# Where transposes stand beside PV, when loads are issued, and how background matmuls run at the end of an attention

## The chip, the cores and the metric

The kernel runs on one core of a Trainium2 chip. The metric is the device time of one execution in microseconds (us); the median of the runs counts. The engines named here are TensorE (PE; its weight loads are PEld), VectorE (DVE), ScalarE (ACT), GpSimd (POOL) and SyncE (SP), which issues nearly all DMAs.

## What is computed

One transformer block with adaptive layer norm, all in float32, over 2048 rows of 512, with 32 heads of 16 and a hidden layer of 1792:

```python
mod = (_silu(c) @ w_mod).reshape(c.shape[0], 6, 1, -1)
sa, ca, ga, sb, cb, gb = (mod[:, 0], mod[:, 1], mod[:, 2], mod[:, 3], mod[:, 4], mod[:, 5])
h = _layernorm(x, axis=-1) * (1 + ca) + sa
x = x + ga * _A_ref(h, A_wqkv, A_wo)          # softmax attention, 32 heads, scale 1/4
h = _layernorm(x, axis=-1) * (1 + cb) + sb
x = x + gb * _B_ref(h, B_w1, B_b1, B_w2, B_b2)  # gelu between two dense layers
```

## The kernel before

**Precision and pieces.** A float32 product is made of three: each operand is split into a high and a low part, and high x high, low x high and high x low are added in PSUM. For scores the parts are stacked along the contraction, 48 rows for a head of 16 (50 for the exponent's scores, which also subtract the row maximum). So a score matmul needs only half of the array's 128 rows, and the kernel keeps two row halves of 64 busy at once: matmuls that follow each other on different halves run beside each other. In the code a half is the index `a` or `h`, 0 or 1, and rows start at `a * 64`.

**Units and half-steps.** The attention is cut into 32 units, one for 4 heads and 512 query rows; unit u covers query block u // 8 and head group u % 8. A unit has 16 chunks of 128 keys, so there are 512 half-steps, `half_step(hs)`, and half-step 16u begins unit u. In each, TensorE gets, written out by hand in program order:

- four max scores, `mx_mm` (L390), which VectorE reduces to row maxima (L395). They run 88 ahead of the rest (`LEAD`), so that a unit's maxima are known before its exponentials; `max_rows` sends them through DRAM (`m<-m` L416, then `qst<-m` L422, six ticks later) into the two extra rows of the query tile. A tick of `clock` is one exponential.
- four scores for the exponential, `exp_mm` (L642), which ScalarE evaluates (L649).
- the four PV matmuls of the step before, `pv_step` (L676), each 128 rows by 32 columns.
- background work, six half matmuls (`RUN`): a job is a group of terms that add up in one bank. `bg_mm(h)` issues one term on row half h alone (L276, called from `mm`); the other half of the same rows follows in the next half-step, on the other half of the array. A group has 24 or 36 halves. Two halves may not add to one bank at the same time, so the first of the next half-step waits for an instruction that was `saw`n after the last one: an exponential, or a read of one column of the newest score bank by VectorE (`tick`, L1115).

An ordinary half-step is thus e, mx, then six times a background half and a score of the other half, then PV. Background half h runs beside scores of half 1 - h.

**Background.** `work` yields the jobs: the rest of the QKV projections (`block0`), and for query blocks 0 to 2, as their attention comes done, the output projection, residual and second layer norm (`front`) and the MLP (`feed`, whose gelu is worked out on GpSimd with a tanh on ScalarE, L910 to L921). Block 3 can only follow the attention, in the part after the loop, which also takes what is left of block 2; there gelu is ScalarE's own function (L903). `held` keeps a job for the next half-step.

**Transposes.** V is transposed on TensorE after its projection (`turn_v`, L335, 12 times within the attention), and so are the normed rows of the second layer norm (`trans`, L874; four each for blocks 0, 1 and 2). Each is four 128 x 128 transposes into one bank, evacuated by ScalarE (L340, L876). V's and those of blocks 1 and 2 are queued in `sides`, and a half-step takes one at its start, that is right behind the PV of the half-step before. They take a bank of the ring `mx`, which has three.

**Loads.** `step_start(s)` runs once a step and issues what is due: for unit u + 2 the query tile at step 16u + 6 and four quarters of K at 16u + 6, 8, 12 and 13, for unit u + 1 two halves of V at 16u + 11 and 12.

**The attention's end.** When the 2048 max scores are out, the last 22 half-steps set `ending`: the ring of e gets five banks, and groups that begin now are run by `bg_whole`, all 128 rows in one matmul, two or three in a half-step, behind the four e, which come in pairs of both halves. What is left when the loop ends is finished behind the last PV.

Of the kernel before, what the change touches and what calls it, by code (L numbers as in the profile page):

```python
# [28 lines left out]
NKC = S // P  # L29
NG = H // 4  # L30
NU = NB * NG
# [29 lines left out]
RUN = 6  # L61
# [9 lines left out]
def block_kernel(ctx: ExitStack, tc: tile.TileContext, x, wqkv, wo, w1, b1, w2, b2, c, w_mod, out):  # L71
# [56 lines left out]
    tick = const.tile([P, 1], F32, name="tick")  # L128
# [146 lines left out]
    def mm(ps, term, i, n, r=slice(None)):  # L275
        return te.matmul(ps, term[0][r], term[1][r], start=i == 0, stop=i == n - 1)  # L276
# [354 lines left out]
    def exp_mm(a, bk="e", behind=False):  # L631

        s, p = divmod(ec[a], 2)
        while begun[0] < min(ec) // 2 + 1:
            begun[0] += 1
            step_start(begun[0] - 1)
        ec[a] += 1
        u, kc = divmod(s, NKC)
        assert u in mrows, (u, ec, xc, red, clock["t"])
        r0 = a * 64  # L640
        ps = take(bk)
        ins = te.matmul(ps, kh(u, kc // 8)[r0 : r0 + KX, p, (kc % 8) * P : (kc % 8 + 1) * P], qst[u][r0 : r0 + KX, p],  # L642
                        start=True, stop=True)
        if behind:
            tc.add_manual_dep(ins.ins, exps[-2].name, AFTER, reason="orders the slots of the exponentials")

        def act():
            t = ppool.tile([P, TB], F32, tag="p", name="p")
            op = ac.activation(t, ps, AF.Exp, scale=SCALE)  # L649
# [162 lines left out]
    def front(b, x2):  # L812
# [9 lines left out]

        def norm(t):
            xn[t] = tmp("xn")
            (gp if t < 3 else ve).tensor_scalar(
                xn[t], x2[t], mv[:, t, 0:1], rs[t], op0=ALU.subtract, op1=ALU.mult)
            later(40, lambda: gp.tensor_tensor(x2[t], x2[t], b2_b, op=ALU.add))
            if b and len(xn) == 4:
                later(9, lambda: sides.extend([lambda fc=fc: trans(fc, "mx") for fc in range(KC)]))
# [25 lines left out]
        for t in range(4):  # L855

            def evac(ps, t=t):
                y = tmp("y")
                ac.activation(y, ps, AF.Copy)

                def add():
                    gp.tensor_tensor(x2[t], y, x2[t], op=ALU.add)
                    later(4 if t < 3 else 3, lambda: stat(t))

                later(2, add)

            yield o_terms(b, t, range(KC)), "bg", evac
# [146 lines left out]
    def saw(ins):  # L1014

        if act["g"] and not act["g"]["seen"]:
            act["g"]["seen"] = ins.ins
# [18 lines left out]
            act["g"] = None  # L1036
        return act["g"] is not None

    def bg_whole():

        g = act["g"]
        terms, bk, evac = g["group"]
        if g["n"] == 0:
            g["ps"] = take(bk)
        mm(g["ps"], terms[g["n"]], g["n"], len(terms))
        g["n"] += 1
        if g["n"] == len(terms):
            evac(g["ps"])
            act["g"] = None
        return act["g"] is not None  # L1050

    held, ending = [], []

    def half_step(hs):
# [4 lines left out]
        h = hs % 2  # L1059
        if h or len(wt) < len(used) + KC:  # L1060
            wload()
        if sides:
            sides.pop(0)()
        full, turn = False, None
        if act["g"] is None:
            j = held.pop() if held else next(jobs, None)
            if callable(j):
                turn = j
                full = True
                j = next(jobs, None)  # L1070
            if callable(j):
                held.append(j)
            elif j is not None:
                act["g"] = {"group": j, "at": [0, 0], "n": 0, "seen": None, "whole": bool(ending)}
        nx = min(64 * NU, LEAD + 4 * (hs + 1))
        ne = 4 * (hs + 1)

        def x_ok(a):
            return sum(xc) < nx and xc[a] < 32 * NU
# [1 line left out]
        def e_ok(a):  # L1081
            return sum(ec) < ne and ec[a] < 2 * NU * NKC

        more = act["g"] is not None
        if more and turn:
            turn()
            turn = None
        free = not more and not full and not ending
        if more and act["g"]["whole"]:
            while sum(ec) < ne:  # L1090
                for f in [exp_mm(a) for a in range(2) if e_ok(a)]:
                    f()
            for _ in range(2 if hs % 3 else 3):
                if act["g"]:
                    bg_whole()
            more = False
        k = 0
        first = more and x_ok(1 - h) and e_ok(h)
# [25 lines left out]
        while sum(ec) < ne or sum(xc) < nx:  # L1124
            a = 0 if ec[0] <= ec[1] else 1
            fs = []
            if sum(ec) < ne:
                fs.append(exp_mm(a))
                if x_ok(1 - a):
                    fs.append(mx_mm(1 - a, "bg" if free and sum(xc) == nx - 1 else "mx"))  # L1130
                elif e_ok(1 - a):
                    fs.append(exp_mm(1 - a))
            else:
                fs += [mx_mm(i) for i in range(2) if x_ok(i)]
            for f in fs:
                f()
            if turn and sum(ec) == ne - 1:
                turn()
                turn = None
        if hs:  # L1140
            assert not turn
            assert min(ec) >= 2 * cur["pv"] + 2
            pv_step()
# [5 lines left out]
    def step_start(s):  # L1149
        u, kc = divmod(s, NKC)  # L1150
        for d in [d for d in due if d[0] <= s and all(k in stored for k in d[1])]:
            due.remove(d)
            d[2]()
        if kc == 0 and u + 2 < NU:
            g = (u + 2) % NG // 2
            due.append((16 * u + 6, [(0, g, (u + 2) // NG)], lambda: load_q(u + 2)))
            for b, n in enumerate((6, 8, 12, 13)):
                t0 = b % 2 * TB
                due.append((16 * u + n, [(1, g, b)], lambda b=b, t0=t0: load_k(u + 2, b // 2, t0, t0 + TB)))
        if kc == 0 and u + 1 < NU:  # L1160
# [9 lines left out]
    if act["g"] and not act["g"]["whole"]:  # L1170
        while bg_mm(1 - hs % 2):
            pass
    pv_step()
    while act["g"]:
        bg_whole() if act["g"]["whole"] else bg_mm(hs % 2)
    close(ppcm, vgcm)


# [128 lines left out]
```

## Time and profile before

| what | value |
|---|---|
| median of 3 runs | 1701.78 us (1700.27 to 1702.31) |
| the profiled execution's own time | 1702.86 us |
| its span, first to last instruction | 1701.1 us |
| mean granted TensorE clock | 0.996 |
| stretch ahead of the attention, 0 to 113 us: PE, DVE, ACT busy | 102.0, 100.6, 39.1 us |
| attention, 113 to 1524 us: PE, DVE, ACT, POOL busy | 1405.2, 1260.5, 1121.3, 589.5 us |
| its end without max scores, 1524 to 1579 us | 54.9, 2.1, 50.1, 34.1 us |
| behind the attention, 1579 to 1701 us | 117.0, 41.2, 26.1, 23.3 us |

In the rows of a timeline stand the start, the time from start to end, the engine, the line, the operation, out<-in, the shape (rows*columns of the array, then partitions x elements) and how many were merged; a bracket holds the idle time ahead and what ended it. A group's row has the busy time, the mean of one in ns, and the idle time ahead with what ended it. A row of the waits view has the total, the count and the longest. Matmuls overlap, so what a matmul costs is read from the distance of starts, not from its own length.

### The profile page before, as it was taken

Reading aid. Unit: us, or ns where it says so; the run is one execution under the profiler, and the core shown is the slowest. Engines: PE = TensorE matmul, PEld = TensorE weight load, DVE = VectorE, ACT = ScalarE, POOL = GpSimd, SP = SyncE. Lnnn points to the kernel's source line nnn. Section 1 sums busy time; section 2 is a strip of 40 time slices with the busy share of each in tenths; the row PEclk is TensorE's granted clock in tenths of the full one; section 3 lists DMA queues with packets and bytes.
Section 4 is the critical chain, followed back from the end, with each engine's and each line's share of the span. In section 5 each row is a group of like instructions: output and inputs, shape, how many; then the busy total and the mean of one; then the engine's idle time right before and its main releaser. Section 6 shows DMA issues by size and latency. Waiting matters only on the chain.

```text
span 1701.1 us, 32616 instructions
## 1 busy us (share of the span) xinstructions
PE 1679.1 (99%) x12097; PEld 919.4 (54%) x12097; DVE 1404.4 (83%) x2677; ACT 1236.7 (73%) x2379; POOL 701.7 (41%) x710
## 2 busy tenths in 40 slices
PE   7999999999999999999999999999999999999999
PEld 6655555555554455555545555555555555553777
DVE  7998888889889988988989888888899888870432
ACT  3358788778777788778777788778777788779131
POOL 7424443435211466316633356316523367136410
PEclk8999999999999999999999999999999999999999
DMA  8746776766457533425463354354363454332554
GB/s 289 200 141 219 228 209 205 222 191 215 129 157 213 128 99 101 107 65 158 133 166 95 94 157 120 83 132 125 107 184 84 124 145 121 68 104 94 189 168 158
DMA packets 137131, 251.91 MB, mean 148 GB/s; under 512 B 25854, under 2 KB 45324, under 8 KB 136972
## 3 DMA queue, kind: packets, MB, share of 16 engines
q1 hardware_dynamic: 135712, 248.19, 51.1%
q8 instruction: 96, 1.57, 0.4%
q10 hardware_dynamic: 1260, 1.63, 0.3%
q14 instruction: 63, 0.52, 0.1%
HBM read 188.49 MB, written 61.28 MB: 147 GB/s over the span
## 4 chain that ended last, share of the span: by engine, by line
PE 92%; DVE 4%; DMA 2%; POOL 1%; ACT 1%; issue 0%; SPq 0%; DVEq 0%; POOLq 0%; ACTq 0%
PE bg L276 38%; PE pv L676 29%; PE e L642 16%; PE mx L390 4%; DVE mxp L395 3%; PE pr L276 2%; DMA wraw<-in_A_wqkv_dram 1%; PE o L276 1%; DMA qst<-m 0%; DMA wt<-wos 0%; ACT p L649 0%; PE mx L335 0%; PE mx L874 0%; DVE hTlo L484 0%; DMA xin<-in_A_x_dram 0%
## 5 line engine op out<-in xcount | busy, mean ns | idle before, releaser
L395 DVE TENSOR_REDUCE mxp<-mx 128x1 f32<-128x512 f32 x2035 | 1285.9, 683 | 146.3 <-PE mx L390 130.2
L649 ACT ACTIVATE p<-e 128x512 f32<-128x512 f32 x2048 | 1074.2, 605 | 274.8 <-PE mx L390 234.2
L390 PE MATMUL mx<-kh,qst 48*128 48x512 f32 x2035 | 833.2, 422 | 1.8 <-DVE mxp L395 1.5
L642 PE MATMUL e<-qst,kh 50*128 50x512 f32 x2048 | 772.4, 425 | 3.9 <-ACT p L649 2.8
L642 PEld LDWEIGHTS e<-qst,kh 50*128 50x128 f32 x2048 | 336.6, 185 | 430.2 <-ACT p L649 308.1
L676 PE MATMUL pv<-p,vg 128*32 128x512 f32 x4096 | 546.8, 605 | 0.0
L390 PEld LDWEIGHTS mx<-kh,qst 48*128 48x128 f32 x2035 | 367.4, 185 | 15.9 <-DVE mxp L395 10.4
L276 PE MATMUL bg<-w,g 64*128 64x512 f32 (+1 forms) x1056 | 265.3, 390 | 0.0
L276 PEld LDWEIGHTS bg<-w,g 64*128 64x128 f32 (+1 forms) x1056 | 195.7, 186 | 28.9 <-POOL m L412 0.2
L676 PEld LDWEIGHTS pv<-p,vg 128*32 128x32 f32 x4096 | 81.4, 108 | 176.5 <-issue 165.5
L276 PE MATMUL bg<-pchi,w 64*128 64x512 f32 (+1 forms) x640 | 175.2, 392 | 0.1
L276 PE MATMUL bg<-hThi,wqkv 64*128 64x512 f32 x560 | 153.0, 392 | 0.1
L276 PEld LDWEIGHTS bg<-pchi,w 64*128 64x128 f32 (+1 forms) x640 | 117.3, 186 | 22.6 <-issue 5.4
L276 PEld LDWEIGHTS bg<-hThi,wqkv 64*128 64x128 f32 x560 | 103.8, 185 | 14.0 <-DVE tick L1115 0.4
L937 POOL TENSOR_TENSOR x<-y,x 128x512 f32<-128x512 f32 x28 | 36.0, 1285 | 166.9 <-ACT y L936 162.5
L918 POOL TENSOR_SCALAR s<-s 128x512 f32<-128x512 f32 x42 | 62.8, 1495 | 99.4 <-ACT s L916 99.3
L276 PE MATMUL bg<-pclo,w 64*128 64x512 f32 (+1 forms) x320 | 87.3, 389 | 0.0
L276 PE MATMUL bg<-hTlo,wqkv 64*128 64x512 f32 x280 | 76.5, 392 | 0.0
L911 POOL TENSOR_TENSOR s<-h 128x512 f32<-128x512 f32 x42 | 43.7, 1040 | 67.3 <-ACT h L910 67.2
L276 PEld LDWEIGHTS bg<-pclo,w 64*128 64x128 f32 (+1 forms) x320 | 58.7, 184 | 9.7 <-issue 2.2
L276 PE MATMUL bg<-wo,pchi 64*128 64x512 f32 x192 | 59.6, 390 | 0.5 <-DVE mxp L395 0.4
L276 PEld LDWEIGHTS bg<-hTlo,wqkv 64*128 64x128 f32 x280 | 51.6, 184 | 7.4
(164 smaller groups left out, 1335.5 us busy)
## 6 DMA issues: line engine op xcount, KB each, us to landing
kh<-qk SPq DMA_DIRECT2D x256, 192.0 KB
w<-w1s SPq DMA_DIRECT2D x56, 512.0 KB
w<-w2s SPq DMA_DIRECT2D x54, 512.0 KB
vg<-v SPq DMA_DIRECT2D x64, 332.0 KB
qk<-parts SPq DMA_DIRECT2D x32, 512.0 KB
qst<-qk SPq DMA_DIRECT2D x64, 192.0 KB
qk<-parts SPq DMA_DIRECT2D x32, 256.0 KB
ou<-osb SPq DMA_DIRECT2D x32, 256.0 KB
```

The costliest lines, as they stand in the source:

```text
L276: return te.matmul(ps, term[0][r], term[1][r], start=i == 0, stop=i == n - 1)
L390: te.matmul(ps, qst[u][r0 : r0 + KR, p, qc * P : (qc + 1) * P], kh(u, kr // 2)[r0 : r0 + KR, p, (kr % 2) * TB : (kr % 2 + 1) * TB], start= ...
L395: ins = ve.tensor_reduce(mxp[u][:, hc, kr : kr + 1], ps, axis=AX.X, op=ALU.max, negate=True)
L642: ins = te.matmul(ps, kh(u, kc // 8)[r0 : r0 + KX, p, (kc % 8) * P : (kc % 8 + 1) * P], qst[u][r0 : r0 + KX, p], start=True, stop=True)
L649: op = ac.activation(t, ps, AF.Exp, scale=SCALE)
L676: te.matmul(cur["ps"][32 * j : 32 * (j + 1)], vg[u][:, kc, j * VW : j * VW + 32], pt.pop(4 * s + j), start=kc == 0, stop=kc == NKC - 1)
L911: gp.tensor_tensor(s, h, h, op=ALU.mult)
L918: gp.tensor_scalar(s, s, 1.0, None, op0=ALU.add)
L937: later(4, lambda: gp.tensor_tensor(x2[t], y, x2[t], op=ALU.add))
```

## The change

**Transposes.** A half-step takes its entry of `sides` at its end, ahead of PV, and not in a half-step in which a group ended. TensorE's order in the eighth half-step, where a transpose of V (L335, four) stands beside PV (L676, four); `-` is before, `+` now:

```order
 L276 MATMUL bg<-hThi_216,wqkv_222 128x512
 L390 MATMUL mx<-kh_193,qst 128x512
-L676 MATMUL pv<-p,vg 32x512 x4
 L335 MATMUL mx<-ident,vr 128x128 x4
+L676 MATMUL pv<-p,vg 32x512 x4
 L642 MATMUL e<-qst,kh_191 128x512
 L390 MATMUL mx<-kh_193,qst 128x512
```

The four transposes moved from behind PV to ahead of it. All 12 of V and the 8 of blocks 1 and 2 move so; the four of block 0 were jobs of their own and stay.

**Halves in balance.** A group no longer starts in a half-step of h = 1 while both halves have issued equally many e; it is held for the next one. Without that rule, in such a half-step three e go to one half, and one of them is of the step after. In half-steps without background the bank `bg` is now lent to the third max score rather than the fourth.

**The attention's end.** `bg_whole` is gone. The first half-step of the end issues six e, the later ones four, so that e run two further ahead; each half-step has four background halves of half h, with an e of the other half behind each. In the last five half-steps no group begins; a fetched one is held until after the loop. VectorE reads a column of the last e's bank (`tick`) for the order of the two halves. TensorE's order in two half-steps of the end before, PV (L676), e (L642) and background (L276):

```order
L676 MATMUL pv<-p,vg 32x512 x4
L642 MATMUL e<-qst,kh_192 128x512 x4
L276 MATMUL bg<-pchi_5392,w_22651 128x512 x2
L676 MATMUL pv<-p,vg 32x512 x4
L642 MATMUL e<-qst,kh_192 128x512 x4
L276 MATMUL bg<-pchi_5392,w_22651 128x512 x3
```

And one now, with each e by its own bank's number, from the last PV matmul to the next first:

```order
L676 MATMUL pv_22433<-p_22799,vg_21764 32x512
L276 MATMUL bg_22803<-pchi0_5392,w1_21633 128x512
L642 MATMUL e_22857<-qst_21150,kh1_191 128x512
L276 MATMUL bg_22803<-pchi0_5392,w1_21633 128x512
L642 MATMUL e_22862<-qst_21150,kh1_191 128x512
L276 MATMUL bg_22803<-pchi0_5392,w1_21633 128x512
L642 MATMUL e_22867<-qst_21150,kh1_191 128x512
L276 MATMUL bg_22803<-pchi0_5392,w1_21633 128x512
L642 MATMUL e_22872<-qst_21150,kh1_191 128x512
L676 MATMUL pv_22433<-p_22826,vg_21764 32x512
```

Whole background matmuls behind the e became halves between them. There are 17 half-steps like this, then three of four e, one of two and one of none, all without background, and 24 whole matmuls (two groups) behind the last PV, where there were 10.

**Loads.** Query tile at 16u + 4, K at 16u + 5, 8, 14 and 16, V at 16u + 2 and 3. SP's order from the store of unit 24's maxima (L416) to their load (L422), before; L362 is K, L595 V, L715 and L718 the attention's sums and output, L791 weights:

```order
L416 DMA m_116<-m_17887 4x32x32 x2
L362 DMA kh_191<-qk_87 48x2x512 x2
L595 DMA vg<-v 128x664
L715 DMA dn<-ou_126 128x1x32
L718 DMA ob<-ou_126 64x1x512 x2
L791 DMA wo<-wos_135 128x1024
L362 DMA kh_191<-qk_87 48x2x512 x2
L422 DMA qst<-m_116 2x1024 x2
```

And now:

```order
L416 DMA m_116<-m_17854 4x32x32 x2
L715 DMA dn<-ou_126 128x1x32
L718 DMA ob<-ou_126 64x1x512 x2
L422 DMA qst<-m_116 2x1024 x2
L791 DMA wo<-wos_135 128x1024
L715 DMA dn<-ou_126 128x1x32
L718 DMA ob<-ou_126 64x1x512 x2
L362 DMA kh_191<-qk_87 48x2x512 x2
```

K and V moved out from between the store and the load.

**Statistics.** In blocks 1 and 2 of `front` the statistics start eight ticks behind the residual addition rather than four or three, and the fourth normalization is GpSimd's like the other three, not VectorE's.

The core of the diff:

```diff
-        ps = take(bk)
+        cur["e"] = ps = take(bk)
...
-            (gp if t < 3 else ve).tensor_scalar(
+            (gp if b or t < 3 else ve).tensor_scalar(
...
-                    later(4 if t < 3 else 3, lambda: stat(t))
+                    later(8 if b else 4 if t < 3 else 3, lambda: stat(t))
...
-        if sides:
-            sides.pop(0)()
...
-            if callable(j):
+            if callable(j) or j is not None and (hs > NU * NKC - RUN if ending else h and ec[0] == ec[1]):
                 held.append(j)
             elif j is not None:
-                act["g"] = {"group": j, "at": [0, 0], "n": 0, "seen": None, "whole": bool(ending)}
+                act["g"] = {"group": j, "at": [0, 0], "n": 0, "seen": None}
...
-        ne = 4 * (hs + 1)
+        ne = min(4 * NU * NKC, 4 * (hs + 1) + 2 * len(ending))
...
-        if more and act["g"]["whole"]:
-            while sum(ec) < ne:
-                for f in [exp_mm(a) for a in range(2) if e_ok(a)]:
+        if more and ending:
+            a = 1 - h
+            if ne - sum(ec) > 4:
+                for f in [exp_mm(i) for i in (h, a) * 2]:
                     f()
-            for _ in range(2 if hs % 3 else 3):
+            k = RUN - 2
+            while k > 0 or sum(ec) < ne:
                 if act["g"]:
-                    bg_whole()
+                    bg_mm(h)
+                if k <= ne - sum(ec):
+                    f = exp_mm(a if e_ok(a) else h)
+                    if act["g"] and sum(ec) == ne:
+                        saw(ve.tensor_copy(tick, cur["e"][:, :1]))
+                    f()
+                k -= 1
             more = False
...
-                    fs.append(mx_mm(1 - a, "bg" if free and sum(xc) == nx - 1 else "mx"))
+                    fs.append(mx_mm(1 - a, "bg" if free and sum(xc) == nx - 2 else "mx"))
...
+        if sides and not (had and act["g"] is None):
+            sides.pop(0)()
         if hs:
...
-            due.append((16 * u + 6, [(0, g, (u + 2) // NG)], lambda: load_q(u + 2)))
-            for b, n in enumerate((6, 8, 12, 13)):
+            due.append((16 * u + 4, [(0, g, (u + 2) // NG)], lambda: load_q(u + 2)))
+            for b, n in enumerate((5, 8, 14, 16)):
...
-                due.append((16 * u + 11 + h, need, lambda h=h: load_v(u + 1, h)))
+                due.append((16 * u + 2 + h, need, lambda h=h: load_v(u + 1, h)))
...
-    while act["g"]:
-        bg_whole() if act["g"]["whole"] else bg_mm(hs % 2)
...
+    for j in held:
+        do(j)
```

More of the change, by code (lines that the diff above doesn't have):

```diff
@@ L1037, in bg_mm @@
         return act["g"] is not None
[L1039 to L1050, printed above, removed]
     held, ending = [], []
@@ L1082, in e_ok @@
             return sum(ec) < ne and ec[a] < 2 * NU * NKC
-        more = act["g"] is not None
+        more = had = act["g"] is not None
         if more and turn:
@@ L1169, in block_kernel @@
         half_step(hs)
-    if act["g"] and not act["g"]["whole"]:
-        while bg_mm(1 - hs % 2):
-            pass
+    assert not act["g"]
     pv_step()
-    while act["g"]:
-        bg_whole() if act["g"]["whole"] else bg_mm(hs % 2)
     close(ppcm, vgcm)
```

## Prediction

> **What bounds the kernel now.** I read the page first.
>
> ```profile
> PE 1679.1 (99%) x12097; PEld 919.4 (54%) x12097; DVE 1404.4 (83%) x2677; ACT 1236.7 (73%) x2379; POOL 701.7 (41%) x710
> ...
> L395 DVE TENSOR_REDUCE mxp<-mx 128x1 f32<-128x512 f32 x2035 | 1285.9, 683 | 146.3 <-PE mx L390 130.2
> L649 ACT ACTIVATE p<-e 128x512 f32<-128x512 f32 x2048 | 1074.2, 605 | 274.8 <-PE mx L390 234.2
> ...
> L276 PEld LDWEIGHTS bg<-w,g 64*128 64x128 f32 (+1 forms) x1056 | 195.7, 186 | 28.9 <-POOL m L412 0.2
> ```
>
> TensorE is busy 99% of the span, so a gain must come from better packed matmuls or from its few waits. The group rows give the mean of one reduction (683 ns), one exponential (605) and one weight load of the background (186). Half-steps are the unit to count in. The timeline of TensorE shows one with four transposes of background b = 1 in it, and then an ordinary one; each ends where the next PV starts.
>
> ```profile
> 953.08 1.07 PE L676 MATMUL pv<-p,vg 128*32 128x512 f32 x8
> 954.08 0.66 PE L874 MATMUL mx<-ident,xn 128*128 128x128 f32 x4
> ...
> 956.82 1.06 PE L676 MATMUL pv<-p,vg 128*32 128x512 f32 x8
> 957.81 0.49 PE L642 MATMUL e<-qst,kh 50*128 50x512 f32 x1
> ...
> 959.34 0.40 PE L390 MATMUL mx<-kh,qst 48*128 48x512 f32 x1
> 959.66 0.64 PE L676 MATMUL pv<-p,vg 128*32 128x512 f32 x4
> ```
>
> The ordinary half-step takes 959.66 - 956.82 = 2.84 us: 0.99 from PV to the first pair of score matmuls, then pairs, then 0.32 from the last max score to PV. The one with transposes takes 3.74, so 0.90 more. TensorE's order holds 450 ordinary ones, 8 such, and 12 with V's transposes, which take 3.55:
>
> ```profile
> 133.02 1.07 PE L676 MATMUL pv<-p,vg 128*32 128x512 f32 x8
> ...
> 136.57 1.07 PE L676 MATMUL pv<-p,vg 128*32 128x512 f32 x8
> ```
>
> ScalarE's timeline in the same two half-steps says why 0.90 and not less. After PV it idles 0.78 us; with transposes there, their evacuation (0.78) stands ahead of the exponentials, the score banks come free later, and pairs fall apart.
>
> ```profile
> 954.83 0.78 ACT L876 ACTIVATE h<-mx,modc 128x512 f32<-128x512 f32 x1 [1.01 <-PE mx L874]
> 955.51 2.05 ACT L649 ACTIVATE p<-e 128x512 f32<-128x512 f32 x4
> 958.34 2.07 ACT L649 ACTIVATE p<-e 128x512 f32<-128x512 f32 x4 [0.78 <-PE mx L390]
> ```
>
> **Transposes ahead of PV.** The number of switches between row shapes stays: scores, transposes, PV, scores instead of scores, PV, transposes, scores. The price at the new place is in a stretch before the attention, where transposes follow a score and precede a matmul of PV's shape.
>
> ```profile
> 79.27 0.41 PE L390 MATMUL mx<-kh,qst 48*128 48x512 f32 x2
> 79.61 0.66 PE L335 MATMUL pr<-ident,vr 128*128 128x128 f32 x4
> 80.20 1.50 PE L232 MATMUL pr<-wm,s_m 128*32 128x512 f32 x12
> ```
>
> A score to a transpose is about 0.33, as a score to PV; the four and the switch behind them are 80.20 - 79.61 = 0.59. So the half-step becomes 2.84 + 0.59 = 3.43. The evacuation now runs while PV does, in the 0.78 us that ScalarE has. What is late next is the bank: the transposes take the score bank of three max scores ago, that is of the second max score of this half-step, and VectorE must have reduced it.
>
> ```profile
> 958.38 1.89 DVE L395 TENSOR_REDUCE mxp<-mx 128x1 f32<-128x512 f32 x3 [0.59 <-PE mx L390]
> ```
>
> Three reductions of 0.68 in 1.89 us start 0.60 apart, so the second ends at 958.38 + 0.60 + 0.68 = 959.66, and the transposes could start at 959.34 + 0.33 = 959.67. That is a tie; I put 0.03 us on it. The bounds are no wait (3.43) and the third reduction's end, 0.60 more (4.03, slower than now); I take 3.46, since the order names the second bank. V: 12 x (3.55 - 3.46) = 1.1 us. Background: 8 x (3.74 - 3.46) = 2.2 us.
>
> **Attention's end.** Here the max scores are used up. Before, e come in pairs, and then two or three background matmuls of all 128 rows:
>
> ```profile
> 1533.16 0.73 PE L642 MATMUL e<-qst,kh 50*128 50x512 f32 x4
> 1533.82 0.73 PE L276 MATMUL bg<-pchi,w 128*128 128x512 f32 x2
> 1534.48 1.06 PE L676 MATMUL pv<-p,vg 128*32 128x512 f32 x8
> ```
>
> From e to PV are 1.32 us, and with the 0.99 from PV to the next e the half-step takes 2.31, for two background matmuls. After, four half matmuls run beside four e. The first half-steps of this stretch show that pairing already:
>
> ```profile
> 1525.18 0.50 PE L276 MATMUL bg<-pchi,w 64*128 64x512 f32 x1
> 1525.18 0.49 PE L642 MATMUL e<-qst,kh 50*128 50x512 f32 x1
> 1525.52 0.39 PE L276 MATMUL bg<-pchi,w 64*128 64x512 f32 x1
> 1525.52 0.62 PE L642 MATMUL e<-qst,kh 50*128 50x512 f32 x2
> 1525.75 0.39 PE L276 MATMUL bg<-pchi,w 64*128 64x512 f32 x1
> ```
>
> First to second pair 0.34, then 0.23. So a half-step is 0.34 + 2 x 0.23 + 0.33 + 0.99 = 2.12 us. The Trainium skill ("TensorE: Matmul & The Clock Gate", Part 3, What overlaps and what doesn't) says that a weight load overlaps a running matmul only when the row group differs; four half matmuls on one half would then each show their load. These rows deny it: 1525.52 and 1525.75 lie on one half, 0.23 apart. It is a rival below.
>
> Now the sum from the first matmul behind the first PV to the first behind the last. Before it is 1579.75 - 1525.18 = 54.6 us.
>
> ```profile
> 1579.75 1.65 PE L276 MATMUL bg<-pchi,w 128*128 128x512 f32 x6
> ```
>
> After, TensorE's order has one half-step of six e (8 slots less two shared, about 2.6), 17 of 2.12 (36.0), three of four e without background (0.34 + 0.33 + 0.99 = 1.66 each, 5.0), one of two e (1.3), and PV alone twice (1.0 + 1.0): 46.9. ScalarE bounds it too, in these rows:
>
> ```profile
> 1532.63 0.70 ACT L910 ACTIVATE h<-bg,b_h 128x512 f32<-128x512 f32 x1
> 1533.20 2.62 ACT L649 ACTIVATE p<-e 128x512 f32<-128x512 f32 x5
> ```
>
> Exponentials start (2.62 - 0.60) / 4 = 0.50 apart here, (2.07 - 0.60) / 3 = 0.49 above, and an evacuation takes 0.57 of its time. 88 e x 0.49 = 43.1, eight other activations x 0.57 = 4.6, the first 0.6 late and the last PV about 1.1: 49.4 if it never idles and all of this must be done by then. Running two e ahead lets it idle little; five banks keep its backlog off TensorE. The two sums give 46.9 to 49.4, and a little above if both wait in turn; I take 48.8, gain 5.8, with 4 to 7 for the range. The added reads of a score bank (L1086 of the new kernel) are on VectorE, whose only other work here is a reciprocal; the background of the next half-step and the last exponential wait for them, but PV's 0.99 lies between. If that cover were gone, each of the 15 would cost a reduction's time at most (683 ns), 10 us in all; a copy of one column is far shorter, and I take nothing.
>
> What is not done here is done later: the order has 24 whole matmuls of two groups behind the last PV, where 10 stood, so 14 more. The chain has their price, and TensorE's timeline where the waiting part begins:
>
> ```profile
> 1619.27 78.23 PE bg L276 x336
> ```
>
> ```profile
> 1597.16 3.07 PE L276 MATMUL o<-wt,kh 128*128 128x512 f32 x11
> ```
>
> 78.23 / 336 = 0.233. From 1579.75 to the output projection at 1597.16 are 17.4 us with 70 matmuls; with 84 it is 19.6. So 2.2 are given back; 0.83 of waits in the 17.4 go, because the last groups' gelu comes from ScalarE rather than GpSimd. Net gain of the end: 5.8 - 2.2 = 3.6.
>
> **Balance, loads, statistics.** The half-step ahead of the attention's end is broken today:
>
> ```profile
> 1520.92 1.07 PE L676 MATMUL pv<-p,vg 128*32 128x512 f32 x8
> 1524.18 1.07 PE L676 MATMUL pv<-p,vg 128*32 128x512 f32 x8
> ```
>
> It takes 3.26; the new order has an ordinary one there (2.84): 0.4 saved. Two kinds of wait follow, in TensorE's timeline:
>
> ```profile
> 880.18 0.47 PE L276 MATMUL bg<-wo,pchi 64*128 64x512 f32 x1 [0.41 <-DVE mxp L395]
> ...
> 1217.05 0.47 PE L642 MATMUL e<-qst,kh 50*128 50x512 f32 x1 [1.07 <-DMA qst<-m]
> ```
>
> At 1217.05 an e of unit 24 waits for its row maxima, because groups had started on the odd half and one e came half a step early; with the pairing that is lost I count 1.5 us, and 1.07 is the lower bound. In balance that e comes later, and K, V and `wo` no longer stand between the store and this load on SP: 1.5 saved. At 880.18 a group waits 0.41 for its bank, which held the last max score; now the one before. This happens twice, and the lost pair goes with it: 0.8. VectorE waits for a GpSimd addition, twice, 0.33 each:
>
> ```profile
> 928.99 0.43 DVE L839 BATCH_NORM_STATS2 bsh<-x 128x6 f32<-128x256 f32 x1 [0.33 <-POOL x L862]
> ```
>
> Eight ticks of delay instead of four cover that: 0.5. The norm moved to GpSimd (two of 2 us, GpSimd 41% busy) costs nothing, nor do V and q loaded earlier.
>
> Sum: 1.1 + 2.2 + 3.6 + 0.4 + 1.5 + 0.8 + 0.5 = 10.1 us. The profiled execution took 1702.86 (span 1701.1), 1.1 above the median; the same off both gives 1692.8 there, and a predicted median of 1701.78 - 10.1 = 1691.7.
>
> **Rivals.** (a) Transposes bound: the 0.90 and 0.71 are the matmuls' own, or the bank wait eats the gain. For it: the tie at 959.66. Against: ScalarE's row. Without 3.3 the time is 1695.0. (b) The end stays ScalarE's: exponentials and evacuations with no overlap, and waits for gelu in the tail; gain 1 of 3.6: 1694.3. (c) Weight loads on one half show: three of 0.186 in each of 17 half-steps, 9.5 us, and the time is 1701.2, no change. For it: four half matmuls lie on one half in a row. Against it: the 0.23 of the rows at 1525.52 and 1525.75. (This is the rule of the Trainium skill quoted above.) (d) It does not do what it says for the loads: unit 24 still waits, or unit 31, whose first e now comes two e sooner: 1.5 to 3 us, 1693.2 to 1694.7. (e) Slower: K's third quarter is now asked for at 16u+14 and used by max scores from 16u+18, four half-steps, 11.4 us. The chain shows a small load taking 7.8.
>
> ```profile
> 1209.12 7.80 DMA qst<-m
> ```
>
> From 11.4 on every unit stalls; a landing after 12 us would cost 0.6 in each of 30 units, 18 us, and the time would be 1709.7. Against it: the first quarter has four half-steps today, and no wait for it is in any view.
>
> **Numbers.** Forecast 0.60, (a) 0.12, (b) 0.13, (c) 0.04, (d) 0.07, (e) 0.04. The forecast's own bounds are 4 to 7 for the stretch and 1 to 4 for transposes: 1689 to 1694; (a), (b) and (d) end by 1695, and two of them together by 1697. So 1688.5 to 1696.5. About 0.2%, 3.4 us, is what can be told from no change: faster 0.92, same 0.04, slower 0.04.
>
> **What would show it.** Right: half-steps with transposes of 3.4 to 3.5 us, ScalarE's evacuation during PV; 17 of 2.1 at the end, and 19.6 us from the last PV to the output projection; no waits at units 24 and at b = 1, 2. Wrong: transposes that wait for VectorE, e that wait for exponentials at the end, a wait for kh.

## The result, and the profile after

The changed kernel takes 1692.54 us in the median of six runs (1691.62 to 1693.95), the kernel before 1701.24 beside it (1700.01 to 1702.31): a ratio of 0.9949, 95% interval 0.9937 to 0.9961. That is 8.7 us less (6.6 to 10.7 by the interval); forecast were 10.1, and 1691.7.

The profiled execution took 1691.76 us (span 1690.0), 11.1 less than the profiled one of before. Of these, 1.6 are not the change's: the first PV starts at 111.35 instead of 112.92, and up to there TensorE, VectorE, ScalarE and GpSimd have the same instructions; only SP issues three loads sooner. In the 14 traces of this study the first PV starts between 110.8 and 113.9 us, with loads at the old steps as with the new. I therefore count from the first PV to the end of the span: 1588.2 us before, 1578.6 after, **9.5 less**. The same measure serves for every experiment below.

The page's row for the engines, then the half-steps with transposes, as TensorE's timeline of the changed kernel has them (start us, duration, engine, line, operation, operands):

```profile
PE 1670.4 (99%) x12121; PEld 919.3 (54%) x12121; DVE 1402.7 (83%) x2692; ACT 1238.0 (73%) x2379; POOL 692.0 (41%) x698
```

```profile
948.05 1.07 PE L676 MATMUL pv<-p,vg 128*32 128x512 f32 x8
...
950.57 0.40 PE L390 MATMUL mx<-kh,qst 48*128 48x512 f32 x1
950.96 0.65 PE L874 MATMUL mx<-ident,xn 128*128 128x128 f32 x4
951.54 1.04 PE L676 MATMUL pv<-p,vg 128*32 128x512 f32 x5
```

951.54 - 948.05 = 3.49 us where 3.74 stood. From the last max score to the transposes are 0.39, where the prediction had 0.33 without a wait, and from there to PV 0.58. ScalarE's timeline at the same place:

```profile
951.71 0.78 ACT L876 ACTIVATE h<-mx,modc 128x512 f32<-128x512 f32 x1
953.07 2.06 ACT L649 ACTIVATE p<-e 128x512 f32<-128x512 f32 x4 [0.58 <-PE mx L390]
```

The evacuation (951.71 to 952.49) runs while PV does, and ScalarE still idles 0.58 before the four exponentials.

At the attention's end, a half-step of the new kind:

```profile
1539.17 1.07 PE L676 MATMUL pv<-p,vg 128*32 128x512 f32 x8
1540.16 0.49 PE L276 MATMUL bg<-pclo,w 64*128 64x512 f32 x1
1540.17 0.50 PE L642 MATMUL e<-qst,kh 50*128 50x512 f32 x1
1540.50 0.39 PE L276 MATMUL bg<-pclo,w 64*128 64x512 f32 x1
...
1540.73 0.39 PE L276 MATMUL bg<-pclo,w 64*128 64x512 f32 x1
...
1541.29 1.07 PE L676 MATMUL pv<-p,vg 128*32 128x512 f32 x8
```

It takes 2.12 us, and its half matmuls, all on one half of the rows, start 0.34 and then 0.23 apart: no weight load (186 ns) shows. So the rule of the Trainium skill ("TensorE: Matmul & The Clock Gate", Part 3, What overlaps and what doesn't) is not borne out here, and rival (c) is refuted.

Now the stretch at the attention's end. I count it from 0.99 us behind the start of the PV at 1516.43, where the first matmul would follow without a wait (it starts at 1517.82), to the first matmul behind the last PV. The view of busy time in this window (length; PE, PEld, DVE, ACT, POOL busy; clock, share of the DMA engines, GB/s), and ScalarE's timeline in it, of the changed kernel:

```profile
1517.42:1566.87 49.45, 48.87 (x349) 19.10 (x345) 3.30 (x19) 47.84 (x97) 33.01 (x33) 1.00 0.30 93
```

```profile
1518.35 4.03 ACT L649 ACTIVATE p<-e 128x512 f32<-128x512 f32 x8 [0.58 <-PE e L642]
1522.19 0.70 ACT L916 ACTIVATE s<-s 128x512 f32<-128x512 f32 x1
1522.71 8.53 ACT L649 ACTIVATE p<-e 128x512 f32<-128x512 f32 x17
1531.11 0.70 ACT L910 ACTIVATE h<-bg,b_h 128x512 f32<-128x512 f32 x1
...
1562.53 3.31 ACT L649 ACTIVATE p<-e 128x512 f32<-128x512 f32 x6
```

The stretch fell from 54.57 to 49.45 us. Between 1518.35 and 1565.84 no row of ScalarE has an idle time, and it counts as busy for 47.84 of 49.45 us. But records of exponentials overlap (each is at least 0.59 long), so a short wait shows only in the distance of their starts. The eight from 1518.35 to 1522.19 start 0.48 apart, as most in the stretch do; the seventeen from 1522.71 to 1531.11 start 0.49 apart on average, because at 1527.54 and 1529.66 an exponential came 0.53 and 0.68 behind the one before it, within 0.1 of its own score's end. There are five such places behind the first exponential; the others start 0.14 to 1.6 behind the end of their scores. What lies beyond 0.48 between exponentials adds up to 0.75 us, where it was 5.6 in the kernel before. So ScalarE sets the length but for some 0.7 us in which it waits for TensorE, and the chain that ended last runs through exponentials for part of the stretch only:

```profile
1522.89 8.35 ACT p L649 x17
```

In the same stretch of the kernel before, ScalarE waits in front of most fours, and part of that shows as idle time:

```profile
1545.60 2.06 ACT L649 ACTIVATE p<-e 128x512 f32<-128x512 f32 x4 [0.16 <-PE e L642]
```

Behind the last PV the waits for GpSimd are gone, but the projection starts later:

```profile
1566.87 2.11 PE L276 MATMUL bg<-pchi,w 128*128 128x512 f32 x8
...
1586.46 11.07 PE L276 MATMUL o<-wt,kh 128*128 128x512 f32 x48
```

1586.46 - 1566.87 = 19.59 us where 17.41 stood: 2.18 given back. The 48 matmuls of the projection take 11.07 us; in the kernel before they took 0.4 more, with no wait that the timeline names (the seventh and eighth started 0.49 and 0.34 behind the one ahead, the others about 0.23):

```profile
1597.16 11.48 PE L276 MATMUL o<-wt,kh 128*128 128x512 f32 x48
```

### The profile page after: what moved, and what is told of

Same layout as the page of the kernel before. It is cut to its first block, busy times and chain, and to the rows that moved or that the text cites. A ratio compares the mean times of both kernels' runs of the same rounds, so it can differ in the third digit from the quotient of the medians.

```text
span 1690.0 us, 32259 instructions
## 1 busy us (share of the span) xinstructions
PE 1670.4 (99%) x12121; PEld 919.3 (54%) x12121; DVE 1402.7 (83%) x2692; ACT 1238.0 (73%) x2379; POOL 692.0 (41%) x698
## 4 chain that ended last, share of the span: by engine, by line
PE 91%; DVE 4%; DMA 2%; ACT 2%; issue 0%; POOL 0%; SPq 0%; POOLq 0%; ACTq 0%; DVEq 0%
PE bg L276 40%; PE pv L676 29%; PE e L642 16%; PE mx L390 4%; DVE mxp L395 3%; ACT p L649 1%; DMA kh<-qk 1%; PE pr L276 1%; PE o L276 1%; PE warm L441 1%; PE mx L335 0%; DVE bst L237 0%; DMA qst<-qk 0%; PE mx L874 0%; DMA qk<-parts 0%; DMA wraw<-in_A_wqkv_dram 0%
## 5 line engine op out<-in xcount | busy, mean ns | idle before, releaser
L642 PE MATMUL e<-qst,kh 50*128 50x512 f32 x2048 | 777.9, 424 | 3.7 <-ACT p L649 3.6
L642 PEld LDWEIGHTS e<-qst,kh 50*128 50x128 f32 x2048 | 341.4, 185 | 429.6 <-ACT p L649 309.8
L676 PE MATMUL pv<-p,vg 128*32 128x512 f32 x4096 | 546.3, 605 | 0.3 <-ACT osb L663 0.3
L276 PE MATMUL bg<-w,g 64*128 64x512 f32 (+1 forms) x1056 | 264.3, 389 | 0.1
L276 PEld LDWEIGHTS bg<-w,g 64*128 64x128 f32 (+1 forms) x1056 | 196.0, 186 | 29.7 <-issue 0.5
L276 PE MATMUL bg<-pchi,w 64*128 64x512 f32 (+1 forms) x656 | 177.8, 391 | 0.0
L676 PEld LDWEIGHTS pv<-p,vg 128*32 128x32 f32 x4096 | 81.0, 108 | 171.7 <-issue 159.0
L276 PE MATMUL bg<-hThi,wqkv 64*128 64x512 f32 x560 | 153.1, 392 | 0.1
L276 PEld LDWEIGHTS bg<-pchi,w 64*128 64x128 f32 (+1 forms) x656 | 120.8, 185 | 25.6 <-DVE tick L1086 5.9
L276 PEld LDWEIGHTS bg<-hThi,wqkv 64*128 64x128 f32 x560 | 103.8, 185 | 14.1 <-DVE tick L1108 0.4
L276 PE MATMUL bg<-pclo,w 64*128 64x512 f32 (+1 forms) x328 | 88.5, 389 | 0.0
L276 PE MATMUL bg<-hTlo,wqkv 64*128 64x512 f32 x280 | 76.5, 392 | 0.0
L276 PEld LDWEIGHTS bg<-pclo,w 64*128 64x128 f32 (+1 forms) x328 | 60.0, 184 | 13.1 <-DVE tick L1086 5.0
L276 PE MATMUL bg<-wo,pchi 64*128 64x512 f32 x192 | 59.3, 388 | 0.0
L411 POOL CAST m<-mt 128x32 fp32r<-128x32 f32 x32 | 6.8, 212 | 121.7 <-DVE mt L409 121.7
```

Of the source, the lines that this page charges most:

```text
L411: gp.tensor_copy(m2[:, 0], mt)
L676: te.matmul(cur["ps"][32 * j : 32 * (j + 1)], vg[u][:, kc, j * VW : j * VW + 32], pt.pop(4 * s + j), start=kc == 0, stop=kc == NKC - 1)
```

## Experiments

Times are medians; a run with no interval was timed once. "From the first PV" is the span less the start of the first PV.

| run | us | beside before: ratio [95%] | from the first PV |
|---|---|---|---|
| before | 1701.24 | | 1588.2 |
| changed | 1692.54 | 0.9949 [0.9937, 0.9961] | 1578.6 |
| transposes_alone | 1698.54 | 0.9987 [0.9978, 0.9996] | 1586.1 |
| short_evac | 1699.66 | | 1585.9 |
| old_end | 1696.02 | 0.9973 [0.9962, 0.9985] | 1581.5 |
| no_lead | 1698.20 | 0.9983 [0.9974, 0.9992] | 1583.7 |
| old_loads | 1691.64 | | 1578.2 |
| no_hold | 1695.41 | | 1581.2 |
| old_loads_no_hold | 1696.65 | | 1581.8 |
| old_stat_bank | 1696.66 | | 1581.0 |
| stat_first | 1690.71 | | 1576.5 |
| end_filled | 1692.36 | 0.9941 [0.9929, 0.9954] | 1577.4 |
| both | 1690.85 | 0.9933 [0.9920, 0.9947] | 1576.2 |
| both_loads | 1690.09 | 0.9933 [0.9918, 0.9947] | 1578.6 |

### Transposes alone

The kernel before, with only this:

```diff
-        if sides:
-            sides.pop(0)()
...
-        more = act["g"] is not None
+        more = had = act["g"] is not None
...
+        if sides and not (had and act["g"] is None):
+            sides.pop(0)()
         if hs:
```

> The kernel before, with nothing changed but the place of the 20 groups of transposes (in front of PV, at the half-step's end). Theory (the evacuation stood ahead of the exponentials on ScalarE and broke the pairs): 12 half-steps go from 3.55 to 3.50 us and 8 from 3.74 to 3.50, together 2.6 us, so about 1698.6 beside 1701.2, and nothing else moves. Rival (the 0.7 to 0.9 us are the matmuls' own): these half-steps stay at 3.55 and 3.74, and the time stays at 1701.2.

1698.54 us, and in TensorE's timeline the same half-step as above:

```profile
950.88 0.66 PE L874 MATMUL mx<-ident,xn 128*128 128x128 f32 x4
951.47 1.07 PE L676 MATMUL pv<-p,vg 128*32 128x512 f32 x8
...
954.96 0.64 PE L676 MATMUL pv<-p,vg 128*32 128x512 f32 x4
```

All twenty half-steps take 3.49 to 3.56 (954.96 - 951.47 = 3.49), 41.9 us together for V and 28.1 for the background instead of 42.7 and 29.9: 2.6 us less, as expected. From the first PV on only 2.0 of this arrive. Some 0.3 are lost at three ends of units, where the half-step that held transposes before now takes 0.09 more than an ordinary one; the rest is spread thinly. The gain stands by itself.

### Evacuation cut short, transposes at their old place

Of the evacuation in batches 1 and 2 only 8 columns are left; this kernel leaves out most of those rows' second layer norm, with a constant in its place:

```diff
-            ac.activation(h, ps, AF.Identity, scale=modc[:, 1, fc, 0:1], bias=modc[:, 1, fc, 1:2])
+            if b:
+                gp.memset(h, 0.5)
+                ac.activation(h[:, :8], ps[:, :8], AF.Identity, scale=modc[:, 1, fc, 0:1], bias=modc[:, 1, fc, 1:2])
```

> The kernel before, with the transposes at their old place, but of those of batches 1 and 2 only 8 of 512 columns are evacuated by ScalarE (the rest of the tile is a constant that GpSimd sets). Theory (ScalarE's 0.78 us ahead of the exponentials is what breaks the pairs): the 8 half-steps fall from 3.74 to 3.4 to 3.5 us. Rival (the transposes' own time and the bank they take): they stay at 3.7.

TensorE and ScalarE at such a half-step:

```profile
947.68 1.07 PE L676 MATMUL pv<-p,vg 128*32 128x512 f32 x8
948.68 0.66 PE L874 MATMUL mx<-ident,xn 128*128 128x128 f32 x4
...
951.12 1.06 PE L676 MATMUL pv<-p,vg 128*32 128x512 f32 x8
```

```profile
949.44 0.36 ACT L878 ACTIVATE h<-mx,modc 128x8 f32<-128x8 f32 x1 [0.50 <-PE mx L874]
949.80 2.06 ACT L649 ACTIVATE p<-e 128x512 f32<-128x512 f32 x4
```

951.12 - 947.68 = 3.44 us: the transposes are where they were, and 0.30 of the 0.90 are gone with 0.42 of ScalarE's evacuation. Six of the eight half-steps take 3.42 to 3.44. The last of each four takes 4.00, and that is the stand-in's doing: GpSimd sets the constant (L877) behind an addition of 1.27 us, and ScalarE waits 1.69 us for it, as its timeline shows:

```profile
953.56 0.36 ACT L878 ACTIVATE h<-mx,modc 128x8 f32<-128x8 f32 x1 [1.69 <-POOL h L877]
```

So ScalarE's evacuation ahead of the exponentials is shown to cause that part; the 0.60 that is left agrees with the 0.59 that the prediction had for four transposes and their switch.

### The old end in the new kernel

The functions of the old end put back, whole matmuls behind the scores, and no score ahead:

```diff
-        ne = min(4 * NU * NKC, 4 * (hs + 1) + 2 * len(ending))
+        ne = 4 * (hs + 1)
...
+        if more and act["g"]["whole"]:
+            while sum(ec) < ne:
+                for f in [exp_mm(a) for a in range(2) if e_ok(a)]:
                     f()
+            for _ in range(2 if hs % 3 else 3):
                 if act["g"]:
+                    bg_whole()
```

> The new kernel with the attention's end as it was (whole background matmuls behind the scores, no score ahead). Theory: from the last half-step with max scores to the last PV 54.6 us again instead of 49.4, but 9 fewer whole matmuls behind the last PV, 2.1 us; 3.1 us slower than the new kernel, about 1695.6. Rival (the end is ScalarE's either way, and the gain of the profiled run is chance): within 1 us of the new kernel, 1692 to 1693.5.

1696.02, 3.5 us slower than the changed kernel. The stretch takes 53.46 us, 4.0 more than after, and the way from the last PV to the projection 17.18, 2.4 less. That it is 53.46 and not 54.57 I put down to the balance rule: the end then starts at a pair, without the three half-steps of 2.59 to 2.71 that finished a half-done group. So up to 1.1 of the 5.1 by which the stretch fell belong to balance; dropping the rule from the changed kernel (no_hold, below) costs the stretch 0.74.

### Halves, but no score ahead

```diff
-        ne = min(4 * NU * NKC, 4 * (hs + 1) + 2 * len(ending))
+        ne = min(4 * NU * NKC, 4 * (hs + 1) + 0 * len(ending))
```

> The new kernel with the end's background still in halves beside the scores, but without the two scores further ahead. Theory (the two scores ahead keep ScalarE from idling early in the stretch, and its exponentials and evacuations bound the stretch): the stretch to the last PV grows by 1 to 2 us, about 1694. Rival (the pairing alone makes the gain, since a half-step is TensorE's 2.12 us): the stretch is as long within 0.5 us, 1692.5.

A miss, of both: 1698.20, 5.7 us slower than the changed kernel; the stretch takes 54.41 us. TensorE's and ScalarE's timelines, and a row each of the list of waits in this stretch (us waited in total, times, longest), here and in the changed kernel:

```profile
1540.54 1.07 PE L676 MATMUL pv<-p,vg 128*32 128x512 f32 x8
1541.54 0.72 PE L642 MATMUL e<-qst,kh 50*128 50x512 f32 x2
...
1542.79 1.54 PE L676 MATMUL pv<-p,vg 128*32 128x512 f32 x8
```

```profile
1540.01 4.19 ACT L649 ACTIVATE p<-e 128x512 f32<-128x512 f32 x8
1544.86 3.69 ACT L649 ACTIVATE p<-e 128x512 f32<-128x512 f32 x7 [0.66 <-PE e L642]
```

```profile
PEld pv L676 <- ACT p L649: 8.9, 21, 0.8
```

```profile
PEld pv L676 <- ACT p L649: 1.0, 3, 0.4
```

PV takes 1.54 instead of 1.06 in every second half-step, and ScalarE idles up to 0.66 behind it. The cause is in the new loop: the half matmuls hold one half of the rows, so all four scores go to the other (`exp_mm(a ...)` with `a = 1 - h`). PV needs two of each half. Without a lead, two of them come from the half-step that PV ends, and PV waits for their exponentials. The two further scores put a half-step's distance between them. What lies beyond 0.48 between ScalarE's exponentials is 5.0 us again, as in the run old_end. So the pairing alone brings nothing to the stretch (54.41 beside 53.46 for the old end); pairing and lead together bring 4.0.

### Loads and balance, one at a time

Loads at their old steps; then the balance rule dropped; then both:

```diff
-            due.append((16 * u + 4, [(0, g, (u + 2) // NG)], lambda: load_q(u + 2)))
-            for b, n in enumerate((5, 8, 14, 16)):
+            due.append((16 * u + 6, [(0, g, (u + 2) // NG)], lambda: load_q(u + 2)))
+            for b, n in enumerate((6, 8, 12, 13)):
...
-                due.append((16 * u + 2 + h, need, lambda h=h: load_v(u + 1, h)))
+                due.append((16 * u + 11 + h, need, lambda h=h: load_v(u + 1, h)))
```

```diff
-            if callable(j) or j is not None and (hs > NU * NKC - RUN if ending else h and ec[0] == ec[1]):
+            if callable(j) or j is not None and ending and hs > NU * NKC - RUN:
```

> The new kernel with q, K and V loaded at the steps of the kernel before, the balance rule kept. If balance alone took away the wait of unit 24 for its row maxima (the score comes half a step, some 1.4 us, later than it did, and the wait was 1.07): no such wait, and the time is 1692.5. If the queue ahead of the load made it: a wait of 1.0 to 1.5 us, 1693.5 to 1694.

> The new kernel without the balance rule, the loads at their new steps. If balance alone took the wait of unit 24 away: the wait of 1.0 to 1.5 us is back. If the queue did: no wait. Either way the half-step ahead of the attention's end is the broken one of 3.26 us again instead of 2.84, 0.4 us, and one of the end's loses its background; 1693 to 1695.

> The new kernel with neither the balance rule nor the moved loads. Both theories: unit 24's wait is back, 1.07 us and a lost pair, 1.5 us in its half-step; 1694 to 1695.5. If it isn't, the wait belonged to something else that the change moved.

Unit 24's wait is back only where both are undone; TensorE's timeline of that run:

```profile
1214.78 0.47 PE L642 MATMUL e<-qst,kh 50*128 50x512 f32 x1 [0.43 <-DMA qst<-m]
```

Its half-step is then 0.85 longer than an ordinary one, less than the 1.5 expected. The size of this delay differs from trace to trace: with neither remedy it is 1.49 in the kernel before, 1.55 in transposes_alone and 0.54 in short_evac. With either remedy alone the half-step takes 2.85. So the moved loads are a second cover for a wait that balance already removes: without them the time from the first PV is 1578.2, no longer than the 1578.6 of the changed kernel. Balance is worth more than forecast. Without it, five half-steps at ends of units are 0.17 to 0.18 longer than ordinary ones, as the same five were in the kernel before (0.08 to 0.12 in the changed one), the broken half-step of 3.27 is back, and the end's stretch takes 50.19: 2.6 us more in all from the first PV on.

### Statistics and the lent bank as before

```diff
-            (gp if b or t < 3 else ve).tensor_scalar(
+            (gp if t < 3 else ve).tensor_scalar(
...
-                    later(8 if b else 4 if t < 3 else 3, lambda: stat(t))
+                    later(4 if t < 3 else 3, lambda: stat(t))
...
-                    fs.append(mx_mm(1 - a, "bg" if free and sum(xc) == nx - 2 else "mx"))
+                    fs.append(mx_mm(1 - a, "bg" if free and sum(xc) == nx - 1 else "mx"))
```

> The new kernel with the old delay of the statistics (4 ticks), the fourth norm of batches 1 and 2 on VectorE, and the bank of a background group lent to the last max score ahead of it instead of the one before. The prediction's terms: 0.8 us for the bank and 0.5 for the statistics, 1.3 more than the new kernel. As the new trace reads: the bank's two waits are back (0.67 and 0.34 over an ordinary half-step), the half-steps of the statistics stay as they are (0.2 to 0.3 over it), 1.0 us more.

2.4 us more from the first PV on; both readings were too small. The bank costs 0.34 twice. Most of the rest is one half-step that took 4.35, 1.51 over an ordinary one (the half-step with these statistics is 0.23 over it in the changed kernel); VectorE, GpSimd and TensorE there:

```profile
1294.99 0.43 DVE L839 BATCH_NORM_STATS2 bsh<-x 128x6 f32<-128x256 f32 x1 [1.55 <-POOL x L862]
```

```profile
1291.61 2.08 POOL L825 TENSOR_SCALAR xn<-x,mv,rt 128x512 f32<-128x512 f32 x1
1293.66 1.30 POOL L862 TENSOR_TENSOR x<-y,x 128x512 f32<-128x512 f32 x1
```

```profile
1296.07 0.49 PE L390 MATMUL mx<-kh,qst 48*128 48x512 f32 x1 [1.04 <-DVE mxp L395]
```

In the new order a norm of 2.08 us stands ahead of the addition on GpSimd, VectorE's statistics wait for it, the reductions wait behind them, and TensorE for those. With the four further ticks and the fourth norm on GpSimd this stall is gone; the run undoes both, so it doesn't say which of them does it.

### The same remedy in batch 0, and a fuller end

Batch 0 has this very stall in both kernels (the 154th half-step behind the first PV, 1.5 us over an ordinary one), and a wait for a norm on VectorE.

```diff
-            (gp if b or t < 3 else ve).tensor_scalar(
+            gp.tensor_scalar(
...
-                    later(8 if b else 4 if t < 3 else 3, lambda: stat(t))
+                    later(8 if b or t == 1 else 4 if t < 3 else 3, lambda: stat(t))
```

> The new kernel with two things more in batch 0: the statistics of its second tile are begun 8 ticks behind GpSimd's addition instead of 4, and its fourth norm is GpSimd's instead of VectorE's. Theory: VectorE's wait of 1.55 us for that addition and the matmul behind it (1.05 us and the lost pair, 1.5 in all) go, and of the 0.44 us wait at the norm, 0.8 with the lost pair, all goes: 2.3 us less, about 1690.2. Rival: GpSimd's norm takes 2.08 instead of 1.05 us, the transposes behind it wait, and a background half-step more is lost: 1.5 less at most, and a half-step there without background.

From the first PV 1576.5, 2.2 less, as expected: the two long half-steps take 2.84 and 2.61 (the second has no background), and TensorE has the same matmuls in every half-step.

```diff
-            if callable(j) or j is not None and (hs > NU * NKC - RUN if ending else h and ec[0] == ec[1]):
+            if callable(j) or j is not None and (hs > NU * NKC - 4 if ending else h and ec[0] == ec[1]):
...
-    assert not act["g"]
     pv_step()
+    while act["g"]:
+        g = act["g"]
+        terms, bk, evac = g["group"]
+        mm(g["ps"], terms[g["at"][0]], g["n"] + 1, 2 * len(terms))
```

> The new kernel, but a background group may still start in the last four half-steps before the end: 16 half matmuls run beside its scores, and 8 whole ones fewer stand behind the last PV. Theory: 8 x 0.233 = 1.9 us less behind the last PV, and 0.4 to 0.9 us more in these half-steps; a gain of 1.0 to 1.5 us, about 1691.3. Rival (the end is ScalarE's alone, and the half matmuls cost nothing): 1.9 less, 1690.6. Rival (the group's banks and its order get in the way of the last PV): no gain.

The stretch with 16 half matmuls more, by the same view of busy time:

```profile
1516.98:1566.43 49.45, 48.88 (x364) 19.87 (x360) 3.93 (x23) 47.83 (x97) 32.99 (x33) 1.00 0.29 93
```

It is 49.45 us again (49.43 to 49.46 in the seven traces with pairing, lead and balance rule). So the 16 half matmuls cost nothing, as the first rival had it: the four half-steps that hold them take 8.49 together instead of 7.78, and TensorE waits that much less for the last exponentials in front of the last PVs. From the last PV to the projection are 17.42, 2.18 less. But 0.9 are lost right behind:

```profile
1583.85 1.81 PE L276 MATMUL o<-wt,kh 128*128 128x512 f32 x6
1585.98 9.82 PE L276 MATMUL o<-wt,kh 128*128 128x512 f32 x42 [0.32 <-DMA wt<-wos]
```

The projection's weights come after it has started. 1692.36 beside a kernel before of 1702.03: a gain over the changed kernel of 1.2 by the trace, and none that the timing can tell.

> The new kernel with the group in the last four half-steps and with batch 0's statistics and fourth norm moved as in the run stat_first: the two gains add, 1.2 and 2.3 us, to about 1689.0. Rival: they do not add, since a later transposition in batch 0 moves the groups that reach the end; 1690 to 1691.

1690.85 us; 1576.2 from the first PV, 2.4 less than the changed kernel, not 3.5: in its trace 1.9 are lost to the weights.

```profile
1583.64 0.85 PE L276 MATMUL o<-wt,kh 128*128 128x512 f32 x3
1585.51 0.96 PE L276 MATMUL o<-wt,kh 128*128 128x512 f32 x3 [1.02 <-DMA wt<-wos]
1586.79 9.83 PE L276 MATMUL o<-wt,kh 128*128 128x512 f32 x42 [0.32 <-DMA wt<-wos]
```

So I sent the weights off earlier:

```diff
         if done[last] < KC - 1:
             try_prep()
-        else:
-            wload()
+        wload()
```

> The kernel of the run named both, and in addition the weight loads behind the last PV are issued one per group of matmuls, so that two of them stand ahead of the store of the reciprocals (rden) on SP and one ahead of its read-back, instead of behind both. Theory (in the run both the output projection waited for its weights, 1.02 and 0.32 us and the unlabelled rest of 1.9 us, because the loads stood behind SP's wait for the reciprocals; so a shorter queue behind the last PV gained nothing): these waits go, from the start of the output projection to the end 103.5 instead of 105.4 us, 1.9 us less than the run both, about 1689.0. Rival (the loads' 512 KB pieces then delay the small transfers of the denominators, and the projection starts later by as much): no gain, 1690.9 or up to 2 us more.

SP's queue in the run before this one (both) and in this one:

```profile
1573.99 0.32 SPq L728 DMA_DIRECT2D rden<-dn  x1
...
1575.48 0.60 SPq L734 DMA_DIRECT2D rb<-rden  x1
```

```profile
1573.99 0.32 SPq L728 DMA_DIRECT2D rden<-dn  x1
1574.35 0.43 SPq L791 DMA_DIRECT2D wt<-wos  x1
1579.18 0.60 SPq L734 DMA_DIRECT2D rb<-rden  x1
```

The rival: the store of the reciprocals and its read-back are 5.19 us apart instead of 1.49, with the loads in flight, and the other three weight loads stand behind the read-back; TensorE waits 2.02 for the first of them. The profiled run is the slowest of its five (1693.45; the others 1689.5 to 1690.2), so what a usual run loses there is open. The median is not to be told from that of both. The fastest version by the traces is both: 0.9933 of the kernel before, and 2.4 us less than the changed kernel, though the two timed intervals overlap. stat_first alone, an edit of two lines, has 2.2 of these.

## Why the prediction was right

**Transposes: 3.3 forecast, 2.6 measured.** The mechanism (evacuation on ScalarE) is shown by two runs. The size: a half-step takes 3.50 instead of 3.46. The transposes do wait for their bank, which was called a tie: 0.06 instead of 0.03, and at 950.96 they start 0.06 behind the end of the second reduction (950.90). 20 half-steps x 0.035 are the 0.7.

**The end: 5.8 forecast, 5.1 measured; given back 2.2 forecast, 2.18 measured.** Between a sum of 46.9 for TensorE and one of 49.4 for ScalarE I took 48.8; the stretch takes 49.45. Two things were wrong there. A value below the larger of two bounds can't be right if the bounds are. And the 49.4 was no bound: it had exponentials 0.49 apart, where most start 0.478 apart, by their single starts in the trace. With the distances of the trace ScalarE needs 48.7: the first exponential 0.93 late, 87 distances of 0.478, 4.3 for the eight other activations, and 1.95 from the last exponential's start to the end. What lies beyond these distances, 0.75 and mostly waits for TensorE, makes up the rest. So it is in part luck that 49.4 agrees with 49.45. The lead of two scores was to keep ScalarE from idling; no_lead shows that without it PV waits as well and nearly the whole gain of the stretch is gone (54.41 beside 54.57 before), so its part was set too low. Rival (b) was right in that ScalarE bounds most of the end, and had the price wrong: that still leaves 5.1.

**Balance, loads, bank, statistics: 3.2 forecast for the four terms, 3.1 measured.** Unit 24: 1.5, as forecast and as the trace of before has it; in the four traces that have this delay it is 0.5 to 1.6. I gave it to balance and loads together; either does it alone. The half-step ahead of the end: 0.4 forecast, 0.6 measured, since the new order has one more half-step without background (2.61) and one ordinary one less. The bank: 0.67 + 0.34 = 1.0 instead of 0.8. Statistics: 0.5 forecast, nothing by the trace: these two half-steps are still 0.31 and 0.23 over. In both, VectorE has the row maxima and work of the statistics one behind the other; the first:

```profile
919.86 0.22 DVE L407 TENSOR_REDUCE mn<-mxp 128x16 f32<-128x64 f32 x1
...
920.25 0.39 DVE L839 BATCH_NORM_STATS2 bsh<-x 128x6 f32<-128x256 f32 x1
```

But without the change to the statistics and the fourth norm one of them would take 1.3 more (4.35 in old_stat_bank, 3.07 here), which the forecast did not see. Not foreseen either: 0.9 in many half-steps, of which 0.3 are at ends of units and 0.2 in one half-step of batch 0; the rest is spread thinly. Against that, one half-step of batch 0 is 0.4 longer.

**Sum.** 2.6 + 5.1 - 2.2 + 3.1 + 0.9 - 0.4, and 0.4 in the output projection, are 9.5, the difference from the first PV on. The terms were each off by up to 0.7, and what was not foreseen (0.9, -0.4 and 0.4) made up for most of it. So the mechanisms held, but that the sum came within 0.6 of the trace is partly luck. The rivals: (c) is refuted by the pitch of 0.23. (d): no wait at unit 24 or 31. (e): no wait for kh in any half-step of the new trace.

## What to carry to other kernels

When two engines each need their own time for a stretch, it takes the larger sum and what they wait for each other on top, not something between. Where records overlap, read the other engine's need and its waits from the distance of starts, not from its idle times: here no row showed an idle time where some 0.7 us were waits. That need says how much the rearrangement can win, and what then rides along free. Work that is paired by halves makes the other work lopsided: ask which of its results are now used in the step that makes them, and give these a lead. A remedy that works at one place (the delay of the statistics) is worth trying wherever the same wait stands in the trace: here it gave 2.2 us more.

## What was not expected of the hardware

With three loads of 512 KB issued from 1570.82 to 1574.78, around a store of 16 KB at 1573.99, the 1.49 us from the reciprocals' store to its read-back became 5.19 in one trace. And the start-up moves by itself: the first PV came between 110.8 and 113.9 us in 14 traces with the same instructions of the computing engines ahead of it, a span of a third of the whole effect of this change.
